# W's tail in two row groups, and the first attention product in two column groups

## The chip, the cores and the metric

The kernel runs on one core of a Trainium2 chip. The metric is the device time of one execution in microseconds (us), compared as the median of timed runs. A core has TensorE (PE, matmuls; its weight loads are listed apart as PEld), VectorE (DVE), ScalarE (ACT), GpSimd (POOL) and SyncE (SP, which here only issues DMAs). Each engine works through its own queue in order, and semaphores order the queues against each other. Matmuls read SBUF and write PSUM; a PSUM bank holds 512 fp32 values on each of 128 partitions. TensorE's array has 128 rows (the contracted dimension) and 128 columns (the output's partitions); a matmul can be given a part of the rows or of the columns.

## The reference

Eight batches, eight heads, 576 tokens, head size 64. Keys and values are averaged in groups of 8 tokens, so that 72 are left per head. The attention's output (576 tokens x 512) goes into a gated MLP:

```
attn = softmax(q @ pool8(k).T / 8);  x = attn @ pool8(v)      # heads side by side: 576 x 512
h = gelu_tanh(x @ w_in);  u, v = h[:, :512], h[:, 512:]
v_n = (v - mean(v)) / sqrt(var(v) + 1e-6) * g_ln
v_s = w_sg @ v_n + b_sg                                       # mixes the 576 tokens
out = x + (u * v_s) @ w_out
```

## The kernel before

Activations stand transposed where they can: features on partitions, 576 tokens along the free dimension, in two halves of 288 (`HALF`), one PSUM bank each. Products of batches 1 to 7, and all products of the MLP, are made of three fp32r products: each operand is split into a high and a low part (`xhl`, `wih`/`wil`, `vhh`/`vhl`, `wsh`/`wsl`, `ghi`/`glo`, `woh`/`wol`), and high x high, high x low and low x high are added up in PSUM. In batch 0 the attention is computed in plain fp32, and an fp32 matmul shows in the trace as two passes, each with a weight load.

The work of a batch is cut into steps, generators named by a letter: A, B, C, E load; K and P pool keys and values; S makes scores and softmax; T and L turn the attention weights (by DMA through HBM in batches 1 to 7, on TensorE in batch 0); V is the attention product for head pair `g`; J (batch 0) and H make the v half of the MLP and normalise it; U makes the u half; W mixes tokens for feature block `d`; O is the output product; Z stores. The long list `ORDER` says in which order the steps advance, each entry up to the step's next `yield`, over all batches. No scheduler reorders: every engine's instructions stand in the order in which this list emits them. The change leaves `ORDER` as it is.

Step W, for feature block `d` (0 to 3, 128 features): the 576 rows of `w_sg.T` are four blocks of 128 and a tail of 64 (`TAIL`). The tail's operands are stacked: `vht` holds the high part of the 64 tail rows of v on partitions 0 to 63 and the low part on 64 to 127, and `wth` holds the high part of W's tail rows twice. One matmul with `wth` so gives high x high and low x high. `wtl` holds W's low part on partitions 0 to 63 and zeros on 64 to 127. Each of the two is multiplied for both halves of tokens: four matmuls of 128 rows and 288 columns at the end of each W step. `vht` is filled at the end of step H for `i` = 4: a cast on ScalarE writes the high part, then a subtraction on VectorE the low part.

Step V of batch 0, for head pair `g`: for each half of tokens, `vb` (128 rows of keys x 128 output columns, 64 for each head) times `ah`, then `vl` times `lt` for the keys that don't fit into 128 rows, added in the same PSUM tile.

Of the kernel before, what the change touches and what calls it, by code (L numbers as in the profile page):

```python
# [8 lines left out]
F32 = mybir.dt.float32  # L9
F32R = mybir.dt.float32r  # L10
# [7 lines left out]
P = 128  # L18
# [76 lines left out]
def tile_pooled_attn_gmlp(ctx: ExitStack, tc: tile.TileContext, q, k0, kv0, v0, k, v, vleft, w_in, w_sg, bg, w_out, out):  # L95
    nc = tc.nc
    B, _, _, S = q.shape
    D = 64
    H = k.shape[2] * 2
    DM = w_in.shape[0]  # L100
    DF2 = w_in.shape[1] // 2
    SP = S // POOL
    NL = 2 * SP - P
    G = H // 2
    KC = DM // P
    NT = -(-S // P)
    TAIL = S - (NT - 1) * P
    HALF = S // 2
# [6 lines left out]
    per = ctx.enter_context(tc.tile_pool(name="per", bufs=1))  # L115
# [7 lines left out]
    def ring(pool, shape, name, bufs):  # L123

        turns[name] = (turns.get(name, -1) + 1) % bufs
        return pool.tile(shape, F32, name=name, tag=f"{name}{turns[name]}")

    def mtile():
        return ring(psm, [P, 2, NB], "mps", 2)

    def atile():
        return ring(psa, [P, 2, NB], "aps", 2)

    def mm(o, lhsT, rhs, start, stop):
        nc.tensor.matmul(o, lhsT, rhs, start=start, stop=stop)  # L135
# [50 lines left out]
    wsl = const.tile([P, NT - 1, S], F32R, name="wsl")  # L186
    wth = const.tile([P, S], F32R, name="wth")
    wtl = const.tile([P, S], F32R, name="wtl")
    nc.gpsimd.memset(wtl.bitcast(F32)[TAIL:2 * TAIL], 0.0)
    both = const.tile([P, S + DF2 // P], F32, name="both")  # L190
    bbc, gcol = both[:, 0:S], both[:, S:]

    st = {}
# [15 lines left out]
    def copy(o, i, key):  # L209
        if key in OTHER:  # L210
            nc.vector.tensor_copy(o, i)
        else:
            nc.scalar.copy(o, i)  # L213
# [18 lines left out]
    def combine(o, x, y, op, key):  # L232
        (nc.vector if key in OTHER else nc.gpsimd).tensor_tensor(o, x, y, op=op)  # L233

    def rest(lo, x, ps, hi, key):
        if key in OTHER:
            nc.vector.tensor_tensor(lo.rearrange("p (a n) -> p a n", a=2), ps,
                                    hi.rearrange("p (a n) -> p a n", a=2), op=ALU.subtract)
        else:
            nc.gpsimd.tensor_tensor(lo, x, hi, op=ALU.subtract)  # L240
# [68 lines left out]
    def step_s(_, c):  # L309
        if c < NT - 1:  # L310
            hi, lo, src = wsh[:, c], wsl[:, c], st["ws", c]
        else:
            hi, lo, src = wth, wtl[:TAIL], st["wt"]
        copy(hi, src, f"s{c}")
        yield
        n = lo.shape[0]
        combine(lo, src[:n], hi[:n].bitcast(F32), ALU.subtract, f"s{c}d")
# [77 lines left out]
    vb = {}  # L395
# [189 lines left out]
    def step_V(b, g):  # L585
        ah, al = st.pop(("a", b, g))
        lt, vl = st["lt", b, g // 2], st["vl", b]
        gl = 2 * (g % 2)
        ps = atile()
        for n in range(2):  # L590
            sl = slice(HALF * n, HALF * (n + 1))
            o = ps[:, n, 0:HALF]
            if b == 0:
                mm(o, vb[b][:, g], ah[:, sl], True, False)
                mm(o, vl[:, g // 2, gl:gl + 2], lt[:, sl], False, True)
                continue
            mm(o, vbh[:, g], ah[:, sl], True, False)
            mm(o, vbl[:, g], ah[:, sl], False, False)
            mm(o, vl[:, g // 2, gl:gl + 2], lt[:, sl], False, False)
            mm(o, vbh[:, g], al[:, sl], False, True)  # L600
        yield
        if ("x32", b) not in st:
            st["x32", b] = dbl.tile([P, KC, S], F32, name="x32")
            st["xhl", b] = (per.tile([P, 2, KC, S], F32R, name="xhl", tag="xhl"),
                            per.tile([P, KC, 2, TAIL], F32R, name="xta"))
        x32, (xhl, xta) = st["x32", b][:, g], st["xhl", b]
        xs, hi = ps[:, :, 0:HALF], xhl[:, 0, g].rearrange("p (a n) -> p a n", a=2)
        copy(hi, xs, f"h{min(b, 3)}{g}")
        copy(x32.rearrange("p (a n) -> p a n", a=2), xs, f"x{min(b, 3)}{g}")
        yield  # L610
        rest(xhl[:, 1, g], x32, xs, xhl[:, 0, g].bitcast(F32), f"V{min(b, 3)}{g}")
        yield
        move(xta[:, g], xhl[:, :, g, S - TAIL:S].bitcast(F32), f"X{min(b, 3)}{g}")
# [13 lines left out]
    def step_H(b, i):  # L627
        by_c = b == 0 and i < NT - 1
        if by_c:
            yield  # L630
        xhl, xta = st["xhl", b]
        xhi, xlo = xhl[:, 0], xhl[:, 1]
        o = st["hp"][i] if by_c else mtile()[:, 0]
        n = min(P, S - i * P)
        t = slice(i * P, i * P + n)
        sl = slice(DF2, 2 * DF2)
        for c in range(0 if by_c else KC):
            if i < NT - 1:
                mm(o, xhi[:, c, t], wih[:, c, sl], c == 0, False)
                mm(o, xhi[:, c, t], wil[:, c, sl], False, False)  # L640
                mm(o, xlo[:, c, t], wih[:, c, sl], False, c == KC - 1)
            else:

                both = (xta[:, c].rearrange("p a t -> p (a t)"), wih[:, c, sl], c == 0, c == KC - 1)
                if c == 0:
                    mm(o, *both)
                mm(o[:n], xta[:, c, 0], wil[:, c, sl], False, False)
                if c > 0:
                    mm(o, *both)
        if not by_c:  # L650
            yield
        vg = ring(per, [P, DF2], "vg", 3)[:n]
        if i == NT - 1:
            nc.scalar.copy(vg, o[n:2 * n])
            yield
            nc.vector.tensor_tensor(vg, o[:n], vg, op=ALU.add)
            yield
            ready(AF.Gelu_apprx_tanh)
            nc.scalar.activation(vg, vg, AF.Gelu_apprx_tanh)
        else:  # L660
            ready(AF.Gelu_apprx_tanh)
            nc.scalar.activation(vg, o, AF.Gelu_apprx_tanh)  # L662
        yield
        bst = per.tile([P, 6], F32, name="bst", tag=f"bst{i}")[:n]
        mv = per.tile([P, 2], F32, name="mv", tag=f"mv{i}")[:n]
        nc.vector.bn_stats(bst, vg)  # L666
        nc.vector.bn_aggr(mv, bst)  # L667
        rstd = per.tile([P, 1], F32, name="rstd", tag=f"rstd{i}")[:n]
        root(rstd, mv[:, 1:2], f"r{min(b, 3)}{i}")
        yield  # L670
        scaled(vg, mv, rstd, f"z{min(b, 3)}{i}")
        yield
        if ("vh", b) not in st:
            st["vh", b] = (per.tile([P, NT - 1, DF2], F32R, name="vhh", tag="vhhi"),
                           per.tile([P, NT - 1, DF2], F32R, name="vhl", tag="vhlo"),
                           per.tile([P, DF2], F32R, name="vht"))
        vhh, vhl, vht = st["vh", b]
        hi, lo = (vhh[:, i], vhl[:, i]) if i < NT - 1 else (vht[0:TAIL], vht[TAIL:2 * TAIL])
        copy(hi, vg, f"g{min(b, 2)}{i}")
        yield  # L680
        if i < NT - 1:
            combine(lo, vg, hi.bitcast(F32), ALU.subtract, f"H{min(b, 2)}{i}")
        else:
            nc.vector.tensor_tensor(lo, vg, hi.bitcast(F32), op=ALU.subtract)

    def halves(ps, pairs, first, last):
        for j, (w, x) in enumerate(pairs):
            for n in range(2):
                mm(ps[:, n, 0:HALF], w, x[:, HALF * n:HALF * (n + 1)], first and j == 0, last and j == len(pairs) - 1)
# [14 lines left out]

    def step_W(b, d):
        vhh, vhl, vht = st["vh", b]
        ps = mtile()
        sl = slice(d * P, (d + 1) * P)
        for c in range(NT - 1):
            halves(ps, [(vhh[:, c, sl], wsh[:, c]), (vhh[:, c, sl], wsl[:, c]), (vhl[:, c, sl], wsh[:, c])],  # L710
                   c == 0, False)
        halves(ps, [(vht[:, sl], wth), (vht[:, sl], wtl)], False, True)
        yield
        u = st.pop(("u", b, d))
        vs = ps[:, :, 0:HALF]
        nc.vector.scalar_tensor_tensor(vs, vs, gcol[:, d:d + 1],  # L716
                                       bbc.rearrange("p (a n) -> p a n", a=2), op0=ALU.mult, op1=ALU.add)
        nc.vector.tensor_tensor(u, vs, u, op=ALU.mult)
        yield
        if ("g", b) not in st:  # L720
            st["g", b] = (per.tile([P, KC, S], F32R, name="ghi", tag="ghi"),
                          per.tile([P, KC, S], F32R, name="glo", tag="glo"))
        ghi, glo = st["g", b]
        uf = u.rearrange("p a n -> p (a n)")
        copy(ghi[:, d], uf, f"G{min(b, 2)}{d}")
        yield
        combine(glo[:, d], uf, ghi[:, d].bitcast(F32), ALU.subtract, f"W{min(b, 2)}{d}")
# [130 lines left out]
```

## Time and profile before

| what | us |
|---|---|
| median of 3 timed runs (lowest, highest) | 547.82 (547.02, 549.65) |
| the profiled execution's own time | 550.16 |
| its span, first to last instruction | 548.5 |
| TensorE matmuls busy | 530.0 (97%) |
| TensorE weight loads busy | 499.9 (91%) |
| VectorE busy | 403.4 (74%) |
| ScalarE busy | 283.4 (52%) |
| GpSimd busy | 263.8 (48%) |

A matmul's time in the profile reaches from its start to its modelled end, and the next one starts before that end: a matmul of 288 columns lasts some 295 ns and its successor starts some 132 ns after it. So what a matmul costs in a stream is read from the distance of two starts, not from its duration. The timeline merges matmuls of the same tiles into one row with a count.

### The profile page before, as it was taken

How to read it: one execution, taken by the hardware profiler on the slowest of the kernel's cores; microseconds unless marked ns; L12 is line 12 of the kernel's file. 1: busy time of each engine (PE TensorE's matmuls, PEld its weight loads, DVE VectorE, ACT ScalarE, POOL GpSimd, SP SyncE). 2: the span in 40 equal slices, each digit the busy share in tenths (PEclk: the TensorE clock that was granted, in tenths of full speed). 3: DMA queues.
4: the chain of work that ended last, by engine and by line, in shares of the span. 5: the costliest groups of instructions: out<-in, count | busy, mean ns of one | idle time of the engine just before them, and what ended most of it. 6: DMA issues, size and time to landing. Idle time of an engine off the chain costs nothing.

```text
span 548.5 us, 9662 instructions
## 1 busy us (share of the span) xinstructions
PE 530.0 (97%) x3600; PEld 499.9 (91%) x3600; DVE 403.4 (74%) x623; ACT 283.4 (52%) x625; POOL 263.8 (48%) x335
## 2 busy tenths in 40 slices
PE   7999888989999999999999999999999999999997
PEld 6877788978999899999989999989999999989997
DVE  3989999879897976798579876776788844754152
ACT  3787974443733955364456755336955744222200
POOL 5567546445474746575356462654247332422121
PEclk9999999899999999999999999999999999999999
DMA  8977014454445365324825255324311323000102
GB/s 316 396 249 270 7 28 147 132 178 145 109 126 159 95 184 154 129 66 113 263 74 168 77 150 163 106 75 114 130 44 50 84 85 107 24 22 2 66 1 86
DMA packets 42655, 67.09 MB, mean 122 GB/s; under 512 B 5232, under 2 KB 21616, under 8 KB 42608
## 3 DMA queue, kind: packets, MB, share of 16 engines
q1 hardware_dynamic: 42320, 66.03, 38.5%
q8 instruction: 28, 0.46, 0.3%
q10 hardware_dynamic: 288, 0.44, 0.2%
q14 instruction: 19, 0.16, 0.1%
HBM read 47.73 MB, written 18.73 MB: 121 GB/s over the span
## 4 chain that ended last, share of the span: by engine, by line
PE 83%; DVE 8%; DMA 4%; ACT 2%; POOL 1%; issue 1%; SPq 0%; ACTq 0%; DVEq 0%; POOLq 0%
PE mps L135 70%; PE aps L135 13%; DMA al<-tfar 1%; DMA kraw<-in_k 1%; DMA tfar<-y 1%; DVE e L459 1%; DVE nmax L507 1%; DVE ssum L478 1%; PE aps L178 1%; DVE bst L666 1%; DVE al L582 0%; DVE aps L457 0%; DVE mv L491 0%; SPq L243 0%; DVE vg L488 0%
## 5 line engine op out<-in xcount | busy, mean ns | idle before, releaser
L135 PE MATMUL mps<-xhl,wih 128*128 128x288 f32 x512 | 89.1, 295 | 1.7 <-ACT vg L662 1.6
L135 PE MATMUL mps<-wih,xhl 128*128 128x512 f32 x256 | 81.3, 398 | 0.0
L135 PEld LDWEIGHTS mps<-xhl,wih 128*128 128x128 f32 x512 | 75.0, 188 | 2.7 <-ACT vg L662 2.0
L459 POOL TENSOR_TENSOR e<-e,ssum 128x720 f32<-128x720 f32 x27 | 40.1, 1487 | 57.3 <-DVE ssum L458 40.7
L233 POOL TENSOR_TENSOR glo<-u,ghi 128x576 fp32r<-128x576 f32 x25 | 37.4, 1504 | 44.4 <-ACT ghi L213 25.1
L135 PEld LDWEIGHTS mps<-wih,xhl 128*128 128x128 f32 x256 | 48.0, 188 | 11.1
L135 PE MATMUL mps<-wsh,vhl 128*128 128x288 f32 x256 | 54.9, 295 | 1.5 <-DVE vhl L233 1.5
L135 PE MATMUL mps<-wsh,vhh 128*128 128x288 f32 x256 | 54.8, 295 | 0.4 <-ACT u L702 0.4
L135 PE MATMUL mps<-xhl,wil 128*128 128x288 f32 x256 | 54.5, 293 | 0.0
L135 PE MATMUL mps<-wsl,vhh 128*128 128x288 f32 x256 | 54.3, 293 | 0.0
L135 PE MATMUL mps<-ghi,woh 128*128 128x288 f32 x244 | 54.0, 301 | 0.0
L135 PE MATMUL mps<-glo,woh 128*128 128x288 f32 x244 | 52.6, 295 | 0.0
L135 PE MATMUL mps<-ghi,wol 128*128 128x288 f32 x244 | 52.5, 295 | 0.0
L240 POOL TENSOR_TENSOR xhl<-x,xhl 128x576 fp32r<-128x576 f32 x23 | 34.4, 1503 | 31.3 <-ACT x L213 15.8
L135 PE MATMUL mps<-wil,xhl 128*128 128x512 f32 x128 | 48.7, 396 | 0.0
L135 PE MATMUL aps<-kbd,qT 128*128 128x144 f32 x300 | 42.3, 291 | 3.4 <-DMA qT<-in_q 1.8
L716 DVE SCALAR_TENSOR_TENSOR mps<-mps,both 128x576 f32<-128x576 f32 x32 | 26.2, 820 | 25.5 <-PE mps L135 25.3
L135 PEld LDWEIGHTS aps<-kbd,qT 128*128 128x128 f32 x300 | 39.7, 192 | 5.1 <-issue 2.0
L206 ACT ACT_TABLE_LOAD x33 | 42.3, 1283 | 0.6
L135 PEld LDWEIGHTS mps<-wsh,vhl 128*128 128x128 f32 x256 | 40.8, 188 | 1.7 <-DVE vhl L233 1.7
L482 POOL TENSOR_TENSOR rstd<-mv,eps 128x1 f32<-128x1 f32 (+1 forms) x40 | 9.8, 245 | 66.1 <-DVE mv L667 65.1
L135 PEld LDWEIGHTS mps<-wsh,vhh 128*128 128x128 f32 x256 | 40.9, 188 | 0.6 <-ACT u L702 0.6
(172 smaller groups left out, 1320.7 us busy)
## 6 DMA issues: line engine op xcount, KB each, us to landing
qT<-in_q SPq DMA_DIRECT2D x31, 288.0 KB, 4.0
out<-x SPq DMA_DIRECT2D x31, 288.0 KB, 2.5
kraw<-in_k SPq DMA_DIRECT2D x14, 576.0 KB, 4.8
al<-tfar SPq DMA_DIRECT2D x28, 288.0 KB, 2.8
vraw<-in_v SPq DMA_DIRECT2D x14, 512.0 KB, 5.0
tfar<-y SPq DMA_DIRECT2D x56, 80.0 KB, 1.9
raw<-in_moe_w_in SPq DMA_DIRECT2D x4, 1024.0 KB, 10.4
tfar<-y SPq DMA_DIRECT2D x56, 64.0 KB, 1.8
```

The costliest lines, as they stand in the source:

```text
L135: nc.tensor.matmul(o, lhsT, rhs, start=start, stop=stop)
L178: nc.tensor.transpose(ps[:rows, i * P:(i + 1) * P], src(i), ident if i < NT - 1 else swap)
L206: nc.scalar.activation(early, eps[:, 0:1], func)
L233: (nc.vector if key in OTHER else nc.gpsimd).tensor_tensor(o, x, y, op=op)
L240: nc.gpsimd.tensor_tensor(lo, x, hi, op=ALU.subtract)
L459: (nc.gpsimd if key in OTHER else nc.vector).tensor_tensor(e, e, rec.unsqueeze(3).broadcast_to([P, NT, 2, SP]), op=ALU.mult)
L478: nc.vector.tensor_reduce(out=ssum, in_=e, axis=AX.X, op=ALU.add)
L482: nc.gpsimd.tensor_tensor(rstd, var, eps[:n, 1:2], op=ALU.add)
L507: nc.vector.tensor_reduce(out=nmax, in_=every.rearrange("p s (h k) -> p s h k", h=2), axis=AX.X, op=ALU.max, negate=True)
L666: nc.vector.bn_stats(bst, vg)
L716: nc.vector.scalar_tensor_tensor(vs, vs, gcol[:, d:d + 1], bbc.rearrange("p (a n) -> p a n", a=2), op0=ALU.mult, op1=ALU.add)
```

## The change

Two edits. In step W, the two `wtl` matmuls of feature blocks 0 and 1 become one matmul of 64 rows for each half of tokens: the first half on partitions 0 to 63 (`vht`'s high part times `wtl`), the second on partitions 64 to 127. For the second, a new tile `vhu` holds the high part of v's tail rows, features 0 to 255, on partitions 64 to 127; a new cast on ScalarE writes it, ahead of the subtraction that makes the low part. `wtl` now holds W's low part twice, where it had zeros in the lower half, and the memset of those zeros is gone. Feature blocks 2 and 3 keep their two matmuls of 128 rows. In step V of batch 0, the matmul with `vb` becomes two of 64 output columns, one for each head.

```diff
-    nc.gpsimd.memset(wtl.bitcast(F32)[TAIL:2 * TAIL], 0.0)
...
-            hi, lo, src = wth, wtl[:TAIL], st["wt"]
+            hi, lo, src = wth, wtl, st["wt"]
...
             if b == 0:
-                mm(o, vb[b][:, g], ah[:, sl], True, False)
+                for h in range(2):
+                    r = slice(D * h, D * h + D)
+                    mm(o[r], vb[b][:, g, r], ah[:, sl], True, False)
                 mm(o, vl[:, g // 2, gl:gl + 2], lt[:, sl], False, True)
...
+            st["vhu", b] = per.tile([P, DF2 // 2], F32R, name="vhu")
+            nc.scalar.copy(st["vhu", b][TAIL:2 * TAIL], vg[:, 0:DF2 // 2])
             nc.vector.tensor_tensor(lo, vg, hi.bitcast(F32), op=ALU.subtract)
...
+        vhu = st["vhu", b]
...
-        halves(ps, [(vht[:, sl], wth), (vht[:, sl], wtl)], False, True)
+        halves(ps, [(vht[:, sl], wth)], False, False)
+        if d >= G // 2:
+            halves(ps, [(vht[:, sl], wtl)], False, True)
+        for n, (x, r) in enumerate(((vht, slice(0, TAIL)), (vhu, slice(TAIL, 2 * TAIL))) if d < G // 2 else ()):
+            mm(ps[:, n, 0:HALF], x[r, sl], wtl[r, HALF * n:HALF * (n + 1)], False, True)
```

On TensorE, the end of the first W step of batch 0 and the start of the second (`mps` is the PSUM tile; the last two numbers are output partitions and columns), before:

```order
L135 MATMUL mps<-wsh,vhh 128x288 x2
L135 MATMUL mps<-wsl,vhh 128x288 x2
L135 MATMUL mps<-wsh,vhl 128x288 x2
L135 MATMUL mps<-wth,vht 128x288 x2
L135 MATMUL mps<-wtl,vht 128x288 x2
L135 MATMUL mps<-wsh,vhh 128x288 x2
L135 MATMUL mps<-wsl,vhh 128x288 x2
```

and after:

```order
L135 MATMUL mps<-wsh,vhh 128x288 x2
L135 MATMUL mps<-wsl,vhh 128x288 x2
L135 MATMUL mps<-wsh,vhl 128x288 x2
L135 MATMUL mps<-wth,vht 128x288 x2
L135 MATMUL mps<-wtl,vht 128x288
L135 MATMUL mps<-wtl,vhu 128x288
L135 MATMUL mps<-wsh,vhh 128x288 x2
```

The number of matmuls is the same; one of the pair now reads `vhu`, and both read 64 rows.

On TensorE, the attention product of batch 0 for head pair 2 (`aps` is its PSUM tile, `ah` the turned attention weights), before:

```order
L135 MATMUL mps<-wih,xhl 128x512 x8
L135 MATMUL aps<-ah,vb 128x288
L135 MATMUL aps<-lt,vl 128x288
L135 MATMUL aps<-ah,vb 128x288
L135 MATMUL aps<-lt,vl 128x288
L178 MATMUL aps<-ident,e 128x128 x4
```

and after:

```order
L135 MATMUL mps<-wih,xhl 128x512 x8
L135 MATMUL aps<-ah,vb 64x288 x2
L135 MATMUL aps<-lt,vl 128x288
L135 MATMUL aps<-ah,vb 64x288 x2
L135 MATMUL aps<-lt,vl 128x288
L178 MATMUL aps<-ident,e 128x128 x4
```

Each matmul with `vb` has become two of 64 output columns, with the same 288 tokens.

On ScalarE, where batch 3 fills `vht`, after the change:

```order
L578 CAST ah<-al 128x576
L705 ACTIVATE u<-mps 128x576
L212 CAST vht<-vg 64x512
L705 ACTIVATE u<-mps 128x576
L686 CAST vhu<-vg 64x256
L212 CAST xhl<-aps 128x576
L205 ACT_TABLE_LOAD
```

The new cast stands behind the gelu that follows `vht`, and ahead of the copies of the next attention product; nothing else moves there.

## Rows read from the trace of the kernel before

**Rows 1.** The page: busy time (share) and instructions; granted clock in 40 slices.
```profile
PE 530.0 (97%) x3600; PEld 499.9 (91%) x3600; DVE 403.4 (74%) x623; ACT 283.4 (52%) x625; POOL 263.8 (48%) x335
...
PEclk9999999899999999999999999999999999999999
```
**Rows 2.** Stretches: length, then each engine's busy time (instructions), granted clock, DMA.
```profile
120.00:300.00 180.00, 178.65 (x1215) 169.30 (x1216) 147.26 (x226) 99.93 (x211) 99.96 (x123) 1.00 0.46 135
300.00:545.00 245.00, 245.00 (x1704) 234.70 (x1702) 154.89 (x242) 109.08 (x221) 93.19 (x116) 1.00 0.26 78
```
**Rows 3.** Waits of TensorE: us in total, times, longest.
```profile
PE aps L135 <- DVE lt L561: 2.0, 1, 2.0
```
**Rows 4.** Chain of waits: start us, us, what; last, a row of VectorE's timeline.
```profile
32.58 2.21 PE aps L135 x8
...
53.58 0.61 ACT vg L662
...
54.21 0.69 DVE L666 BATCH_NORM_STATS2 bst<-vg 128x6 f32<-128x512 f32 x1 [0.94 <-ACT vg L662]
```
**Rows 5.** Timeline of TensorE, first tail of W: start us, us, instructions.
```profile
80.73 0.42 PE L135 MATMUL mps<-wth,vht 128*128 128x288 f32 x2
80.99 0.43 PE L135 MATMUL mps<-wtl,vht 128*128 128x288 f32 x2
81.26 0.42 PE L135 MATMUL mps<-wsh,vhh 128*128 128x288 f32 x2
```
**Rows 6.** Timeline of TensorE, pooling of keys in batch 0; last, all passes' durations.
```profile
9.46 0.47 PE L135 MATMUL mps<-pool,raw 64*128 64x112 f32 x2
9.86 1.15 PE L135 MATMUL mps<-pool,kraw 128*128 128x112 f32 x8
10.94 0.47 PE L135 MATMUL mps<-pool,raw 64*128 64x112 f32 x2
...
17.52 0.72 PE L135 MATMUL mps<-pool,kraw 128*128 128x112 f32 x5
...
L135 PE MATMUL mps<-pool,kraw x32: 275/275/363, 8.4 to 18.0; 128*128 128x112 f32 x32
```
**Rows 7.** Timeline of TensorE, tail of H in batch 0: rows*columns of the array.
```profile
57.27 0.40 PE L135 MATMUL mps<-wih,xta 128*128 128x512 f32 x1
57.50 0.39 PE L135 MATMUL mps<-wil,xta 128*64 128x512 f32 x1
57.73 0.39 PE L135 MATMUL mps<-wih,xta 128*128 128x512 f32 x1
```
**Rows 8.** Timeline of TensorE, attention products of batch 0.
```profile
32.58 0.75 PE L135 MATMUL aps<-ah,vb 128*128 128x288 f32 x2 [0.30 <-ACT ah L213]
...
40.38 0.65 PE L135 MATMUL aps<-ah,vb 128*128 128x288 f32 x2
40.87 0.65 PE L135 MATMUL aps<-lt,vl 128*128 128x288 f32 x2
41.35 0.65 PE L135 MATMUL aps<-ah,vb 128*128 128x288 f32 x2
```
**Rows 9.** ScalarE's casts by form (busy, mean ns); its timeline and TensorE's in batch 3.
```profile
L393 ACT ACTIVATE kbd<-kp 64x144 f32<-64x144 f32 x24 | 7.7, 322 | 7.5 <-DVE kp L371 7.4
L435 ACT ACTIVATE vbh<-vp,head 128x256 fp32r<-128x256 f32 x14 | 6.3, 499 | 2.6 <-PE aps L135 2.5
...
278.73 0.62 ACT L213 CAST vht<-vg 64x512 fp32r<-64x512 f32 x1 [4.49 <-DVE vg L488]
279.25 0.64 ACT L702 ACTIVATE u<-mps 128x576 f32<-128x576 f32 x1
...
280.35 0.53 PE L135 MATMUL mps<-wth,vht 128*128 128x288 f32 x2 [1.35 <-DVE vht L684]
280.72 0.43 PE L135 MATMUL mps<-wtl,vht 128*128 128x288 f32 x2
```
**Rows 10.** Timeline of GpSimd at the start.
```profile
8.78 1.27 POOL L233 TENSOR_TENSOR top<-top,wih 128x512 f32<-128x512 f32 x1 [1.60 <-ACT wih L219]
```

## The prediction

> **What bounds the kernel now.** I read the busy shares first, then stretches of the run, then the waits of TensorE and the chain of waits, and last the timeline at the changed places. [rows 1]: TensorE's matmuls are busy 530.0 us of a span of 548.5, and the granted clock is in the top tenth in all slices but one, so it stays at the 2.4 GHz level. [rows 2]: from 120 to 300 us they are busy 178.65 of 180.00 us, from 300 to 545 us all of 245.00. Whatever lengthens TensorE's work there lengthens the run. The waits are nearly all in the first quarter [rows 3]: the longest is 2.0 us, on the small operand `lt` for batch 1. The one after 120 us that counts is for `vht` of batch 3, 1.35 us before 280.35 [rows 9].
>
> Before 100 us the chain changes hands [rows 4]: TensorE carries it from 32.58 on, the gelu on ScalarE follows at 53.58, and then VectorE, which had been idle for 0.94 us when the result came. So a delay of TensorE between 33 and 53 us is handed on by VectorE. Where VectorE, ScalarE and GpSimd carry the chain (from 54.21 on, until the wait for `lt`) TensorE has time to spare; the first two tails of batch 0 fall there (the first at 80.99 [rows 5]).
>
> **The tail of W.** Each feature block of W ends in four matmuls of 128 rows and 288 columns: two with `wth`, two with `wtl`. The pair with `wtl` starts at 80.99 and the next matmul at 81.26, the pair before it at 80.73 [rows 5]: 0.13 us each. In two of the four blocks the `wtl` pair becomes two matmuls of 64 rows, one on rows 0 to 63 and one on rows 64 to 127, into two PSUM banks. That is 2 x 8 = 16 pairs, 14 of them after 120 us; the two of batch 0 I cost at nothing, covered by the slack above (without that cover, two more pairs at the price below).
>
> The most that a pair can save is one matmul, 0.13 us, if the second runs wholly beside the first: 14 x 0.13 = 1.8 us.
>
> Against that stands what a change from 128-row to 64-row matmuls and back costs. The trace shows it in the pooling of batch 0 [rows 6]. Within eight full-height passes of 112 columns the step is 0.11 us: the group of five lasts 0.72 us, one pass 0.275, so (0.72 - 0.275)/4 = 0.111. Two 64-row passes start at 9.46, eight full ones at 9.86, the next two 64-row ones at 10.94. That round trip of ten passes takes 1.48 us and not 10 x 0.111 = 1.11: going into 64-row matmuls and back out costs 0.37 us. These passes are fp32 and both on the same rows; two on different rows stand nowhere in this trace. So the bounds of a pair are: 0.37 more, if the second runs beside nothing; 0.37 - 0.13 = 0.24 more, if it runs wholly beside the first; 0.13 less, if fp32r matmuls change height for nothing. I take 0.24: height is what the pooling rows share with the new pair, and the overlap is what they can't show. 14 x 0.24 = 3.4 us; the ends are 14 x 0.37 = 5.2 and -1.8.
>
> The Trainium skill says the same of the direction and more of the reach: TensorEngine Tiling, "Tiling Modes", has every change of tiling mode (not of tile) drain the engine. For height the rows above agree. For width they don't: in the tail of H full-width and 64-column matmuls alternate at 57.27, 57.50 and 57.73, 0.23 us each [rows 7], and no step is longer. Taken at its word, the rule would charge the eight width changes in and out of the attention product too, another 8 x 0.37 = 3.0 us by the pooling's price; I don't count it.
>
> **The first attention product by heads.** In batch 0 each of 4 head pairs x 2 token halves has one fp32 matmul `aps<-ah,vb` of 128 output columns. It is issued as two passes: two start at 40.38, the next two (`lt,vl`) at 40.87, then two at 41.35 [rows 8], so one pass is (41.35 - 40.38)/4 = 0.243 us. After the change there are two matmuls of 64 output columns, with the same 128 rows and the same 288 tokens, so the same time to stream: four passes for two. In the order of issue they are first head, first head, second head, second head. Two passes of one head use the same columns and can't run beside each other; the second head's first pass may run beside the first head's last. That makes three steps for two, 0.243 us more; nothing beside makes four, 0.487 more; only if the heads' passes pair up fully is it nothing. It cannot be a gain. I take three: 8 x 0.243 = 1.95 us (ends 0 and 3.9). One bit is absorbed: the second product waits 0.30 us at 32.58 for the copy `ah` on ScalarE, which does not depend on the first one's matmuls [rows 8]. 1.95 - 0.30 = 1.65 us; at four steps 3.6.
>
> **The rest.** ScalarE gets one more cast per batch, 64 x 256 values; between the 64 x 144 and the 128 x 256 casts of [rows 9], 0.32 to 0.50 us, some 0.4. ScalarE is busy 283.4 us of 548.5 [rows 1]. The closest place is batch 3: `vht` ends at 279.35, the gelu behind it at 279.89, so the new cast ends near 280.3, and the pair that wants it starts at 280.72 [rows 9]. The copies queued behind it (`xhl<-aps`, `x<-aps`) come 0.4 us later, and their attention tile has a second buffer; if that cover is gone the price is up to 0.4 us in a batch. On VectorE nothing is added. The memset of half of `wtl` goes; after the memsets GpSimd idles 1.60 us, waiting for ScalarE [rows 10], so nothing comes earlier. The split of W's tail rows writes 128 partitions where it wrote 64, with the same elements each: nothing.
>
> **Sum.** 3.4 + 1.65 = 5.05 us on the profiled execution's 550.16 us, 555.2. That execution is 2.3 us above the median of the timed runs, 547.82, so I put the change on the median: 552.9 us.
>
> **Rivals.**
> *The second 64-row matmul does not run beside the first.* Its weights (64 x 128, through the same loader) come only after the first one's. For: in [rows 6] nothing runs beside anything. Against: there both use the same rows. 5.2 + 1.65 = 6.85 us: 554.7.
> *The attention product takes four steps for two*, with the tail as forecast. For: every pair of passes in [rows 8] is in step, one after the other. 3.4 + 3.6 = 7.0 us: 554.8.
> *Not slower: the height change is free for fp32r, and the pair runs at once.* The place is W's tail, the price of a pair -0.13 us, and the point from which it decides is a price of the change below 0.13 us for a pair. For: banks and rows are disjoint, and all the pooling's passes are fp32. Against: 0.37 us is far above 0.13. -1.8 + 1.65 = -0.15 us: 547.7; with an attention product that costs nothing, 546.0. The skill's TensorE: Matmul & The Clock Gate, "Part 3: Packing small matmuls", speaks for this rival: matmuls at different tile positions start some 4 ns apart, and a weight load passes a running matmul where the row groups differ. No run here shows that so far.
>
> **Chances.** Forecast 0.30; tail not beside 0.28 (with either attention product, up to 5.2 + 3.6 = 8.8 us, 556.6); four steps 0.17; free height change 0.25. What this kernel's measurement can tell from no change is about 0.5%, 2.7 us. The first three are all beyond it: slower 0.75. The free case lies between -1.8 and +1.8 us, so same, 0.20; 0.05 is left for faster, for which nothing that I can price is enough: the whole gain of 16 pairs is 2.1 us. The range leaves out the free case's lower part and what lies above 5.2 + 3.6: 547.6 to 556.8.
>
> **What would show it.** Right: in the tail of W, in blocks 0 and 1, the step into the 64-row pair and the ones behind it are longer than 0.13 us, 0.24 to 0.37 in sum over a pair, and blocks 2 and 3 stay as they are; the two 64-row matmuls start closer than a stream of 0.12 us if they run beside each other; the batch-0 product's two halves are 0.73 (three steps) or 0.97 us (four) apart before `lt,vl`. TensorE's waits after 120 us stay as few as they are. Wrong: a pair's two matmuls start together and the next one follows at 0.13 us; then the time stays where it was. Or a wait on `vhu` shows before a pair, which would make the new cast the cause.

## The result, and the profile after

The changed kernel takes 552.54 us (median of 6 runs, 551.03 to 552.98); the kernel before, in the runs shared with it, 547.46. The ratio is 1.0081, with a 95% interval of 1.0056 to 1.0105: slower by 4.4 us (3.1 to 5.7). The two medians are 5.08 us apart, which lies inside that interval; the ratio is not that of the medians. The forecast was 552.9 and slower. Ratios here and below leave out slow runs; there was one, of 2097 us, in the last set of the product with one visit. The page of the changed kernel's profiled execution (552.98 us, span 551.3), to be held against [rows 1]:

```profile
PE 536.1 (97%) x3616; PEld 496.7 (90%) x3616; DVE 402.8 (73%) x623; ACT 287.5 (52%) x633; POOL 263.4 (48%) x334
...
PEclk9999999999999999999999999999999999999999
```

TensorE is busy 6 us longer; sixteen more passes are those of the attention product. The first tail of W, in TensorE's timeline (start, length, instructions), answers to [rows 5]:

```profile
83.38 0.43 PE L135 MATMUL mps<-wth,vht 128*128 128x288 f32 x2
83.74 0.40 PE L135 MATMUL mps<-wtl,vht 64*128 64x288 f32 x1
83.74 0.39 PE L135 MATMUL mps<-wtl,vhu 64*128 64x288 f32 x1
84.07 0.53 PE L135 MATMUL mps<-wsh,vhh 128*128 128x288 f32 x2
84.44 0.43 PE L135 MATMUL mps<-wsl,vhh 128*128 128x288 f32 x2
```

The two 64-row matmuls start together (3 ns apart in the trace). But from 83.38 to 84.44 it is 1.06 us where six full matmuls took 6 x 0.132 = 0.79. The tails of blocks 2 and 3, which the change leaves alone, take what they took before. The weight loads show where it goes:

```profile
83.74 0.18 PEld L135 LDWEIGHTS mps<-wtl,vht 64*128 64x128 f32 x1 [0.17 <-issue]
83.74 0.18 PEld L135 LDWEIGHTS mps<-wtl,vhu 64*128 64x128 f32 x1
84.06 0.30 PEld L135 LDWEIGHTS mps<-wsh,vhh 128*128 128x128 f32 x2
```

Elsewhere the next weights are loaded while a matmul runs. Here the pair's loads start only 0.225 us after the last `wth` matmul instead of 0.132, and both run at once and in the open (the pair's matmuls last 0.40 us and not 0.295); after the pair the same again, 0.325 us to the next matmul and 0.236 to the one behind it. That TensorE first lets the matmuls in flight run dry at each switch is a reading of these gaps: no row shows it, and the modelled end of the last `wth` matmul (83.81) lies behind the pair's start. In sum a pair takes 0.263 us more, and all 14 pairs after 120 us take 0.26 to 0.27 us but one, whose second matmul came another 0.16 us late. Below, a visit is the whole detour: the switch into narrower matmuls, what is done there, and the switch back.

In the batch-0 attention product, answering to [rows 8], the four 64-column passes of one token half stand in one row:

```profile
41.75 0.71 PE L135 MATMUL aps<-ah,vb 128*64 128x288 f32 x4
42.38 0.75 PE L135 MATMUL aps<-lt,vl 128*128 128x288 f32 x2
43.06 0.71 PE L135 MATMUL aps<-ah,vb 128*64 128x288 f32 x4
```

They are two pairs: the heads' first passes start 7 ns apart at 41.75, their second ones 7 ns apart at 42.04. (The records don't name the head. That each pair holds one pass of either head is read from an experiment below, where two passes on the same columns start 0.29 us apart.) Yet from 41.75 to 43.06 a half takes 1.32 us (1.318 in the trace) and not 0.97: the change of width costs 0.35 us.

TensorE's waits from 96 us on are shorter than in the kernel before ([rows 3, 9] and the first line here; the other two are after the change):

```profile
PE aps L135 <- DMA qT<-in_q: 1.8, 1, 1.8
...
PE aps L135 <- DVE lt L560: 1.5, 1, 1.5
...
PE aps L135 <- DMA qT<-in_q: 1.1, 1, 1.1
```

The run is best read in two parts, cut where TensorE restarts behind the wait for `lt`. Stretch from there to TensorE's last matmul, before (length, then TensorE's busy time):

```profile
95.97:545.28 449.31, 445.91 (x3068) 425.59 (x3068) 321.06 (x492) 217.31 (x452) 205.62 (x250) 1.00 0.35 105
```

and after:

```profile
98.63:548.08 449.45, 448.09 (x3068) 423.52 (x3068) 319.69 (x492) 220.72 (x459) 206.05 (x250) 1.00 0.36 105
```

Restart 2.66 us later, 2.18 us more work behind it, 3.40 us of waits there cut to 1.36: 2.66 + 2.18 - 2.04 = 2.8 us, the difference of the two spans. That is less than the 4.4 us of the timed runs, and less work than 14 x 0.263 = 3.7 us, because this execution of the kernel before lost time of its own behind its restart, in the window just after it (the seventh number is the granted clock):

```profile
97.40:100.70 3.30, 3.30 (x16) 3.30 (x15) 2.50 (x4) 2.05 (x5) 2.95 (x3) 0.50 0.60 160
```

The clock stood at 0.50, the 1.2 GHz level, for some 3.3 us after the 1.96 us wait (the 8 in the clock line of [rows 1]); the changed kernel's wait is 1.45 us there and its clock stays at 2.4 GHz.

### The profile page after: what moved, and what is told of

Same layout as the page of the kernel before. It is cut to its first block, busy times and chain, and to the rows that moved or that the text cites. A ratio compares the mean times of both kernels' runs of the same rounds, so it can differ in the third digit from the quotient of the medians.

```text
span 551.3 us, 9699 instructions
## 1 busy us (share of the span) xinstructions
PE 536.1 (97%) x3616; PEld 496.7 (90%) x3616; DVE 402.8 (73%) x623; ACT 287.5 (52%) x633; POOL 263.4 (48%) x334
## 4 chain that ended last, share of the span: by engine, by line
PE 86%; DVE 7%; DMA 3%; ACT 1%; POOL 1%; issue 1%; SPq 0%; DVEq 0%; ACTq 0%; POOLq 0%
PE mps L135 72%; PE aps L135 14%; DMA kraw<-in_k 1%; DMA tfar<-y 1%; DVE e L458 1%; DVE nmax L506 1%; DVE ssum L477 1%; PE aps L178 1%; DMA al<-tfar 1%; DVE bst L667 0%; DVE aps L456 0%; DVE mv L490 0%; DVE al L581 0%; DVE e L463 0%; SPq L242 0%
```

## The experiments

Ratios are to the kernel before in the same session, with 95% intervals.

**W's tail alone.** The attention product is put back.

```diff
-                for h in range(2):
-                    r = slice(D * h, D * h + D)
-                    mm(o[r], vb[b][:, g, r], ah[:, sl], True, False)
+                mm(o, vb[b][:, g], ah[:, sl], True, False)
```

> The tail of W alone is changed; the attention product of batch 0 is as before. In the trace of the whole change a tail with a 64-row pair takes 0.26 us more than one with two 128-row matmuls (0.39 us for going in and out, less 0.13 us for the second matmul, which starts 3 ns after the first). Theory A (that price, paid wherever TensorE bounds): 14 x 0.26 = 3.7 us over the kernel before, ratio 1.0067. Rival B (the change's cost is mostly the attention product's): under 2 us, ratio below 1.0035.

Ratio 1.0056 (1.0037 to 1.0075), 3.1 us (2.0 to 4.1); TensorE's work behind the restart is 448.08 us, as in the whole change. The tail is the larger part of the loss, as theory A has it; rival B's 1.0035 lies just outside. Theory A's 1.0067 lies inside.

**The attention product alone.** The other half of the edit, on the kernel before.

```diff
-                mm(o, vb[b][:, g], ah[:, sl], True, False)
+                for h in range(2):
+                    r = slice(D * h, D * h + D)
+                    mm(o[r], vb[b][:, g, r], ah[:, sl], True, False)
```

> The attention product of batch 0 alone is changed. In the trace of the whole change its eight halves take 1.32 us each and not 0.97, so 8 x 0.35 = 2.8 us, of which 0.2 to 0.3 lie under the wait for the copy. Theory A (VectorE hands the delay on to the end): 2.5 us, ratio 1.0046. Rival B (the delay is taken up by the DMA waits near 112 us, which in the whole change's trace were 0.8 us shorter, and by the wait for the tail's operand at 280 us, 1.3 us shorter): under 1 us, ratio below 1.002.

Ratio 1.0003 (0.9986 to 1.0020). The restart is at 98.43 us, 2.46 us later than before, so the delay does reach it; but the ratio is that of no change, so theory A falls and rival B holds by it. The ratio hides something, though: 9 of the 12 runs have their clock at the full level, and only 7 of the 23 of the kernel before (how this is told stands with the table below). Between the runs at full clock the product costs 1.0 us (0.3 to 1.7; medians 548.21 and 547.25), which is neither theory A's 2.5 us nor nothing. This split was made after the results were known. Its waits behind the restart:

```profile
PE mps L135 <- DVE vht L686: 1.1, 1, 1.1
PE aps L135 <- DMA qT<-in_q: 0.4, 1, 0.4
PE aps L135 <- DVE al L582: 0.2, 1, 0.2
```

**Both matmuls of a pair on rows 0 to 63.**

```diff
-        for n, (x, r) in enumerate(((vht, slice(0, TAIL)), (vhu, slice(TAIL, 2 * TAIL))) if d < G // 2 else ()):
+        for n, (x, r) in enumerate(((vht, slice(0, TAIL)), (vht, slice(0, TAIL))) if d < G // 2 else ()):
```

> As the whole change, but both 64-row matmuls of a pair use rows 0 to 63, and the new cast is gone. Theory A (two on the same rows can't run beside each other; on different rows they do): the pair's second matmul starts 0.23 us after the first (weight load 0.107 in the open, then the first one's 0.12) and not 0.003, and each pair is 0.13 us longer: 14 x 0.13 = 1.8 us over the whole change. Rival B (the 3 ns are only how the records are written, nothing overlaps): the same time as the whole change.

```profile
83.34 0.43 PE L135 MATMUL mps<-wth,vht 128*128 128x288 f32 x2
83.70 0.53 PE L135 MATMUL mps<-wtl,vht 64*128 64x288 f32 x2
84.15 0.53 PE L135 MATMUL mps<-wsh,vhh 128*128 128x288 f32 x2
84.52 0.43 PE L135 MATMUL mps<-wsl,vhh 128*128 128x288 f32 x2
```

The second matmul starts 0.24 us after the first, and from 83.34 to 84.52 it is 1.18 us: 0.12 to 0.13 us more than with two row groups, 0.39 more than before the change. So the overlap is real, and worth just the one matmul that it was meant to save. TensorE's work behind the restart is 449.37 us, 1.3 more than the whole change's. Ratio 1.0090 (1.0072 to 1.0107); the whole change's interval overlaps it, so the difference of the two rests on the traces.

**Three pairs in one visit.** Feature block 0 alone; `vhu` and `vlu` are copies of the high part on partitions 64 to 127 and of the low part on 0 to 63.

```diff
-        halves(ps, [(vht[:, sl], wth), (vht[:, sl], wtl)], False, True)
+            for k, (w, pair) in enumerate(((wth, (vht, vhu)), (wth, (vlu, vht)), (wtl, (vht, vhu)))):
+                for n, (x, r) in enumerate(zip(pair, (top, low))):
+                    mm(ps[:, n, 0:HALF], x[r, sl], w[r, HALF * n:HALF * (n + 1)], False, k == 2)
```

> The kernel before, with the whole tail of feature block 0 (and of that block alone) in 64-row matmuls: three pairs in a row, high x high, low x high, high x low, where there were four 128-row matmuls; the attention product is as before. Theory A (the price is for going in and out, whatever is inside): 3 steps of 0.13 us for 4, plus 0.39, so a tail takes 0.26 us more, as a tail of the whole change does; over 8 tails 2.1 us, at least 1.8 of it outside slack, ratio 1.0035. Rival B (each 64-row pair pays): 3 x 0.26 = 0.79 us more for a tail, 5.5 to 6.3 us in all, ratio 1.011.

```profile
155.07 0.39 PE L135 MATMUL mps<-wth,vht 64*128 64x288 f32 x1
155.08 0.40 PE L135 MATMUL mps<-wth,vhu 64*128 64x288 f32 x1
155.31 0.29 PE L135 MATMUL mps<-wth,vlu 64*128 64x288 f32 x1
155.31 0.29 PE L135 MATMUL mps<-wth,vht 64*128 64x288 f32 x1
155.44 0.29 PE L135 MATMUL mps<-wtl,vht 64*128 64x288 f32 x1
155.45 0.29 PE L135 MATMUL mps<-wtl,vhu 64*128 64x288 f32 x1
155.66 0.53 PE L135 MATMUL mps<-wsh,vhh 128*128 128x288 f32 x2
```

The third pair follows the second after 0.13 us, the step of a full matmul: inside the visit pairs cost nothing extra. Only the first and the last step are long. The tail takes 0.26 us more than four full matmuls, with three pairs as with one (0.26 to 0.28 us in six of the eight batches; in batch 3 TensorE waited for an operand, and in batch 6 one matmul came another 0.3 us late). Theory A; the time, 1.0056 (1.0031 to 1.0080), holds A's 1.0035 and not B's 1.011.

**An fp32 matmul of 64 columns at column 0.**

```diff
+                mm(o[0:D], vb[b][:, g, 0:D], ah[:, sl], True, True)
                 mm(o, vb[b][:, g], ah[:, sl], True, False)
```

> The kernel before, with an extra fp32 matmul of 64 columns at columns 0 to 63 ahead of each of the eight attention products of batch 0; the full matmul that follows overwrites its result. In the tail of H fp32r matmuls of 64 columns at the same place change width at no price; in the changed attention product, fp32 at columns 0 and 64, they pay some 0.35 us. Theory A (what costs is a place other than column 0): the two extra passes cost 2 x 0.243 = 0.49 us a product, 3.6 to 3.9 us in all. Rival B (fp32 at 64 columns pays at column 0 too): 0.49 + 0.35 = 0.84 us a product, 6.4 to 6.7 us in all, and the first full pass behind them starts 0.33 us after the last small one.

```profile
34.38 1.38 PE L135 MATMUL aps<-ah,vb 128*64 128x288 f32 x4 [0.30 <-ACT ah L213]
35.60 0.65 PE L135 MATMUL aps<-lt,vl 128*128 128x288 f32 x2
36.18 1.14 PE L135 MATMUL aps<-ah,vb 128*64 128x288 f32 x3
```

A half takes 36.18 - 34.38 = 1.80 us, 0.83 more than before: rival B. (The row of four merges the two extra passes with the two full ones behind them.) So it is not the place that makes width cost something; fp32 pays at column 0, where the fp32r matmuls of H's tail pay nothing [rows 7]. The type alone does not settle it either: those matmuls stream 512 values a row and not 288, and the kernel before has narrow fp32 work that pays nothing, the transposes of 32 columns at 37.96 (another kind of matmul, so this is a hint):

```profile
37.85 0.27 PE L178 MATMUL aps<-swap,e 128*128 128x128 f32 x1
37.96 0.60 PE L178 MATMUL aps<-ident,el 128*32 128x128 f32 x4
```

The step into them is 0.11 us, as between full ones. What makes a narrow matmul pay stays open. Restart 6.5 us later, but ratio 1.0084 (1.0053 to 1.0116), 4.6 us: some 2 us are given back again. (No run has fp32r matmuls at columns 64 to 127.)

**The product with one visit for both halves.** On the kernel before; the two full matmuls with `lt` follow behind all four.

```diff
+        for n in range(4 if b == 0 else 0):
+            h, n = n % 2, n // 2
+            r = slice(D * h, D * h + D)
+            mm(ps[r, n, 0:HALF], vb[b][:, g, r], ah[:, HALF * n:HALF * (n + 1)], True, False)
...
-                mm(o, vb[b][:, g], ah[:, sl], True, False)
```

> The attention product of batch 0 by heads, as in the change, but the four 64-column matmuls of both token halves stand together and the two full ones behind them; W's tail is as before. Theory A (each going in and out costs some 0.35 us): 4 visits for 8, so the product's cost is 4 x 0.35 = 1.4 us and not 2.8 over the kernel before. Rival B (each 64-column matmul is dearer by itself): 2.8 us as with the product changed alone.

```profile
40.64 1.19 PE L135 MATMUL aps<-ah,vb 128*64 128x288 f32 x8
41.76 1.24 PE L135 MATMUL aps<-lt,vl 128*128 128x288 f32 x4
42.84 0.60 PE L178 MATMUL aps<-ident,e 128*128 128x128 f32 x4
```

Four visits for eight: 42.84 - 40.64 = 2.20 us for both halves (1.94 before the change, 2.54 with a visit for each), so the price is for the visit. The time came out below that of before, 0.9973 (0.9952 to 0.9993), which neither theory had.

**The cast alone.** `vhu` is written and not read.

```diff
+            st["vhu", b] = per.tile([P, DF2 // 2], F32R, name="vhu")
+            nc.scalar.copy(st["vhu", b][TAIL:2 * TAIL], vg[:, 0:DF2 // 2])
```

> The kernel before with the new cast on ScalarE, whose result nobody reads. Theory A (hidden): the same time as before within 0.3 us. Rival B (ScalarE's 8 x 0.4 us show): up to 3 us more.

Ratio 0.9996 (0.9976 to 1.0017); the cast takes 0.40 us and is hidden. Theory A.

**Where the delay before the restart goes.** Four more kernels: a delay of 1 us, as below; one of 2.9 us, with `g >= 1` in its place; the kernel before unchanged; and the product with one visit unchanged.

```diff
             if b == 0:
+                if g >= 3:
+                    mm(o, vb[b][:, g], ah[:, sl], True, True)
```

> The kernel before, with each attention product of head pair 3 in batch 0 computed twice: TensorE is delayed by 2 x 0.49 = 1.0 us at 45 us and nothing else is changed. The product by heads alone delayed it by 2.4 us at the restart behind the wait for lt and measured no longer time; in its profile the waits behind the restart were 1.7 us and not 3.4. Theory A (a later restart finds its data nearer, so the waits behind it shrink by about as much, to some 2 us): within 0.5 us of before. Rival B (a delay before the restart costs in full, and the result of the product alone was chance): 1.0 us more.

> As the 1 us delay, with the products of head pairs 1, 2 and 3 computed twice: 6 x 0.49 = 2.9 us. Theory A: 0.5 to 1.5 us more than before, since some 2 us of waits are all that can be given back (the 6.5 us delay of the extra 64-column matmuls measured 4.4 us). Rival B: 2.9 us more.

> The kernel before, unchanged: what two sets of runs of one program differ by. Every theory: a ratio whose interval holds 1.

> The product by heads with one visit, unchanged, once more with more runs: it measured 0.27% less than before, although its TensorE work is 4 x 0.26 = 1.0 us longer. Theory A (the longer work is given back by shorter waits, no more): a ratio of 0.998 to 1.001. Rival B (it is a faster kernel): 0.997 or less again.

| kernel | restart | TensorE's work behind it | waits behind it | ratio (95%) |
|---|---|---|---|---|
| before | 95.97 | 445.91 | 3.40 | 1 |
| before, again | 95.97 | 444.50 | 1.70 | 0.9991 (0.9968 to 1.0013) |
| 1 us delay | 97.10 | 445.54 | 0.01 | 0.9992 (0.9974 to 1.0010) |
| 2.9 us delay | 99.18 | 445.61 | 0.27 | 1.0026 (1.0008 to 1.0043) |
| product alone | 98.43 | 444.34 | 1.73 | 1.0003 (0.9986 to 1.0020) |
| product, one visit | 96.82 | 444.07 | 0.95 | 0.9973 (0.9952 to 0.9993) |
| the same, again | 96.77 | 445.86 | 0.69 | 0.9970 (0.9951 to 0.9989) |

(Restart, work and waits are from one profiled execution each, in us.) The 1 us delay costs nothing that can be measured and excludes 1.0018; the 2.9 us delay costs 1.4 us (0.4 to 2.4), not 2.9. So a delay ahead of the restart is given back up to some 1.5 us. The waits behind it are for `qT`, which a DMA brings (1.82 us in the kernel before), for `vht`, which VectorE writes (1.35 us, [rows 9]), and for `al` (0.22 us).

The table shows one thing more: the work behind the restart is 444.1 to 444.5 us or 445.5 to 445.9. The higher ones have the 3.3 us at half the clock, so a profile is best held against one of the kernel before at the same clock: 3.40 us of waits where the clock fell, 1.70 where it did not. The two delays, whose clock fell, have 0.01 and 0.27 for 3.40: there the waits did shrink. The product alone, whose clock did not fall, has 1.73 for 1.70: in its profile nothing shrank. In the runs, the mean granted clock of each tells them apart: below 0.999 in 55 of 90 runs of the kernel before (and in 5 of the 12 of "before, again"), in 3 of 12 of the product alone, and in none of 18 runs of the three kernels that have both tails of the change in batch 0 (whole change, tail alone, same rows). In the session of the tail alone, the kernel before has a median of 547.25 us in its 7 runs at full clock and 549.40 in the other 16; the tail alone 551.46 in 6 at full clock, 4.2 us over the like runs of before (3.1 to 5.3). Split in this way, the 1 us delay is 0.4 us above the kernel before in its 4 runs at full clock and 1.3 us below it in the other 8, and the 2.9 us delay 2.4 us above in 3 and 0.6 us above in 9: most of what is given back is given back in runs whose clock fell.

**Order alone.** As the product with one visit, without column groups: the full matmuls of both halves, then those with `lt`.

```diff
+        for n in range(2 if b == 0 else 0):
+            mm(ps[:, n, 0:HALF], vb[b][:, g], ah[:, HALF * n:HALF * (n + 1)], True, False)
...
-                mm(o, vb[b][:, g], ah[:, sl], True, False)
```

> The kernel before with the order of the batch-0 product alone changed: both token halves' full matmuls with vb, then both with lt; no column groups. The product by heads with one visit has this order too and measured 0.3% less than before, twice. Theory A (the order makes it faster): ratio near 0.997. Rival B (the 1 us later restart behind the wait for lt does): no change, 0.999 to 1.001, since TensorE's work and the restart are as before.

Ratio 0.9998 (0.9975 to 1.0021): the order is not what made the one-visit kernel faster. That kernel beats the one before by 0.3% in two sessions, and at either clock (1.3 to 1.8 us between the medians). In its first profile, at full clock, the shorter waits (0.95 for 1.70) only make up for the later restart (0.85 us); in its second, where the clock fell, they shrink by 2.7 us. The 1 us delay is as much faster only in the runs whose clock fell. Why the one-visit kernel is faster at full clock stays open.

## Why the prediction was right, and where it was not

The direction and the time were right; of the two terms one was right for its reason, and the other not.

*The tail of W.* Forecast: 0.24 us for a pair, the second matmul beside the first, the price of the height change as in the pooling [rows 6], 3.4 us. Measured: 0.263 us, 3 ns apart, 14 x 0.263 = 3.7 us of work, and 3.1 us (2.0 to 4.1) in time, 4.2 us (3.1 to 5.3) between runs at full clock. The step from the fp32 pooling to fp32r was sound: a visit costs 0.39 us (same rows), against 0.37. The rival of no overlap is out by the same-rows kernel, the rival of a free height change by every pair. That rival had a row for it which the prediction did not look at: in the kernel before, fp32r matmuls of 96 rows stand between full ones at 0.13 us a step,

```profile
109.77 0.29 PE L135 MATMUL aps<-lt,vl 96*128 96x288 f32 x1
109.90 0.30 PE L135 MATMUL aps<-al,vbh 128*128 128x288 f32 x1
```

so a change of height is free at 96 rows and costs at 64; taking 64-row passes as the model was right. The Trainium skill's TensorE: Matmul & The Clock Gate, "Part 3: Packing small matmuls", has such matmuls start some 4 ns apart; the trace agrees, 3 ns. Its sentence that a weight load passes a running matmul only in another row group fits the pair, whose second load starts with the first matmul at 83.74, but not the stream of full matmuls, where each load of 0.19 us runs beside a matmul on the same rows (one every 0.132 us).

*The batch-0 tails at nothing.* The restart is 0.16 us later with the tail alone (96.13), so they did lie under the slack, but not without effect: two pairs fill 0.52 us of the wait before the restart (1.96 to 1.45 us), and in none of the runs with both of them did the clock fall behind that wait, where it fell in 55 of 90 before. That took back a part of the loss which no term of the forecast had; the prediction had read one slice at 8 in the clock line of [rows 1] as a clock that stays at 2.4 GHz. That the shorter wait keeps the clock up is inferred from these kernels: no run changed the wait alone, and the product alone has the same 1.96 us wait, yet the clock fell in only 3 of its 12 runs.

*The attention product.* This step failed in its parts. Forecast: three steps for two, no price for width, 1.95 us less 0.30, all of it handed on to the end. The passes pair up fully, 7 ns apart, because the passes of the two heads alternate: zero steps more. But width has a price in fp32, 0.35 us for a visit, 8 x 0.35 = 2.8 us. [rows 7], from which I took width to be free, is fp32r with a stream of 512 values a row and not 288, and the fp32 matmul at column 0 shows that it does not carry over. The rule of the Trainium skill that I set aside, TensorEngine Tiling, "Tiling Modes" (a change of mode drains), gave 3.0 us for these visits, by the pooling's price, and came near the 2.8 measured; for fp32r at column 0 the trace still contradicts it. The restart then came 2.46 us later with the product alone, and VectorE handed the delay on up to there as forecast; but not to the end: the run took 0.0% longer (-0.14 to +0.20%), and 1.0 us (0.3 to 1.7) between runs at full clock. So the 1.65 us of the sum came near by errors that cancel: one step of streaming too many, a price for width too few, and a delay of 2.46 us of which only some 1.0 reached the end. Where it went is shown only in part: the delays above lose it in shorter waits, the profile of the product alone does not.

*The rest.* The cast is hidden, 0.40 us each, as forecast. TensorE's waits after 120 us did not grow with the whole change; the one for `vht` of batch 3, 1.35 us in [rows 9], is 0.04 us in the changed kernel's profile. That the sum met the measured 5.08 us of the medians to 0.03 is luck. At full clock the tail cost 4.2 us where the forecast had 3.4, and the product 1.0 where it had 1.65; together they make 5.2 us, and the whole change at full clock stands 5.0 us (4.0 to 6.0) above the 35 such runs of the kernel before in the four later sessions. Between all runs the difference is the 4.4 us of the ratio, since the kernel before loses time to its clock and the changed one does not.

## What to carry to other kernels

Going from full-height to half-height matmuls and back cost 0.39 us here, three full matmuls of 288 columns: by this price row groups pay only where one visit saves more than three such steps, and one pair saves one. Look for the same change of shape elsewhere in the trace before, but of the same kind: 96 rows were free and 64 were not, 64 columns were free in fp32r streaming 512 values and not in fp32 streaming 288. Before charging a delay to the end of the run, look at what TensorE waits for behind it: up to 1.5 us was given back here. And before reading a ratio near 1 as no cost, compare runs at the same granted clock: 1.0 us of the product was hidden by it.

## What the runs showed of the hardware that was not expected

- Two fp32 matmuls on different column groups, issued one after the other with two passes each, run as two pairs (7 ns apart, the next pair 0.29 us later), so, as read above, the second head's first pass came ahead of the first head's second pass.
- A 64-column fp32 matmul at column 0 pays 0.35 us going in and out; 64-column fp32r matmuls that stream 512 values a row at the same place pay nothing [rows 7], nor do 32-column fp32 transposes (0.11 us a step at 37.96).
- fp32r matmuls of 96 rows between full ones pay nothing (0.13 us a step at 109.77); of 64 rows, 0.39 us for a visit.
- Two weight loads for different row groups start at the same time (83.74) and delay neither (0.18 us each).
- The clock fell to the 1.2 GHz level for some 3.3 us behind a wait of 1.96 us. By the mean granted clock it fell in about three of five runs of the kernel before, in 3 of 12 of the product alone with the same wait, and in none of the 18 of the kernels where that wait was 1.2 to 1.5 us in the profile.
